# A planner that lists by latest times, and one more half-norm turned on VectorE, in a transformer layer on one core

## The chip, the cores and the metric

The kernel runs on one core of a Trainium2 chip. TensorE (PE) multiplies matrices, VectorE (DVE), ScalarE (ACT) and GpSimd (POOL) work element by element, and SyncE (SP) issues the DMAs. Each engine works through its own queue of instructions in order. The metric is the device time of one execution in microseconds (us), as a median over runs.

## The reference

A layer of 2048 rows and 640 features in fp32: a norm, attention over 8 keys at a stride of 2 (32 heads of 20), an output projection with a residual, a second norm, and a gated feed-forward network (FFN) of 1728 columns with a residual.

```python
h  = x + attention(layernorm(x), wqkv) @ wo     # keys at pos - 2*w, w = 0..7
h2 = h + (silu(n @ w_gate) * (n @ w_up)) @ w_down    # n = layernorm(h)
```

## The kernel before

The rows are worked in four blocks of 512 (`b` = 0 to 3), each in four groups of 128 rows (`j`). An fp32 product is made of three passes over splits of its operands into a high and a low part: high with high, then the two mixed ones. The high part is usually a copy on ACT, the low part a subtraction on DVE, and a transpose on PE stands ahead of both where columns are wanted.

The stages lie behind one another on PE and beside one another on the other engines: the qkv products of all blocks (L549, 480 columns wide) up to 240 us, with the projection wo(0) of block 0 (L798, 320 wide, groups of 15 matmuls) between 190 and 216 us; then the FFN of block 0 (gate and up L868, down L879, 512 wide), in which wo(1) is placed, and so on for wo(2) and wo(3). In the last part, blocks 2 and 3 share products of sums (L963, L985). The attention itself runs on DVE: products of 128x2560 (L600 and L635), sums (L607, L643), and small steps between. Its outputs are turned back to columns and split (L716, L788) ahead of each projection.

**The second norm of a block.** For every row group, `wo` adds the residual on DVE, takes the sums, forms the reciprocal deviation with short dependent steps on DVE (`rstd`, L363 to L369), and applies it on ACT. For a block in `HALF`, rows 0 and 1 are applied as a pair (`apply_pair`, L328), turned on DVE in one 128x1280 transpose (L384), stored to a scratch in DRAM with four DMAs (L388), loaded back turned (L391), and copied and split in ten pieces of 256 columns (`pair_columns`, L398 and L399); rows 2 and 3 go through ten transposes of 128x128 on PE (L407), with their copies and splits (L409, L410). For a block that isn't in `HALF`, all 20 transposes are PE's (`x_columns`, L442) with five copies (L445) and five splits (L446) of 512 columns. Before the change, `HALF` is blocks 1 and 2.

**What sets the order.** Every step is recorded in a plan with its engine, an estimated cost, what it reads and writes, and a priority number (`P.add`). `order` simulates five engines: whenever one is free, it takes the ready step with the lowest priority number. DVE's attention steps have priority 20, and wait if a step with priority 1 or less is to be ready before they would end. The start times that come out are shifted by hand for some steps (`SHIFT`, 50 entries), and the steps are emitted by these times, a step never ahead of one it depends on. What is emitted is the order of every engine's queue; no engine changes it at run time.

Of the kernel before, what the change touches and what calls it, by code (L numbers as in the profile page):

```python
# [23 lines left out]
NF = 14  # L24
# [4 lines left out]
HALF = (1, 2)  # L29
# [5 lines left out]
LAT, LAT0, RATE = 4.0, 2.0, 350e3  # L35
# [11 lines left out]
class Plan:  # L47
# [23 lines left out]
    def order(self):  # L71
        ops = self.ops
        left = [len(o[3]) for o in ops]
        succ = [[] for _ in ops]
        for n, o in enumerate(ops):
            for d in o[3]:
                succ[d].append(n)
# [7 lines left out]
        bus, loaded, start = 0.0, None, [0.0] * len(ops)  # L85
        todo = len(ops)
        while todo:
            best = None
            for e in pend:
                if ready[e]:  # L90
                    t = free[e]
                elif pend[e]:
                    t = max(free[e], pend[e][0][0])
                else:
                    continue
                if best is None or t < best[0]:
                    best = (t, e)
            t, e = best
            while pend[e] and pend[e][0][0] <= t:
                m = heapq.heappop(pend[e])[1]  # L100
                heapq.heappush(ready[e], (ops[m][4], m))
            prio, n = ready[e][0]
            if e == "PE" and prio >= 10:
                soon = min((a for a, m in pend[e] if ops[m][4] == PR["wo0"]), default=1e9)
                if soon < t + 0.3:
                    free[e] = soon
                    continue
            if prio >= 20:
                soon = min((a for a, m in pend[e] if ops[m][4] <= 1), default=1e9)
                if soon < t + ops[n][1] - 0.3:  # L110
                    free[e] = soon
                    continue
            heapq.heappop(ready[e])
            todo -= 1
            _, cost, _, _, _, table, nbytes = ops[n]
            if table is not None and table != loaded:
                cost, loaded = cost + 1.3, table
            start[n] = t
            free[e] = t + cost
            end = t + cost  # L120
            if e == "SP":
                bus = max(bus, end) + nbytes / RATE
                free[e] = max(free[e], bus - 3.0)
                end = bus + (LAT0 if ops[n][4] == 0 else LAT)
            for m in succ[n]:
                same = ops[m][0] == e and e != "SP"
                avail[m] = max(avail[m], end + (0.0 if same else 0.2))
# [3 lines left out]
        self.end = max(free.values())  # L131
        self.start = start
        left = [len(o[3]) for o in ops]
        key = [(t + SHIFT.get(n, 0.0), n) for n, t in enumerate(start)]
        heap, out = [key[n] for n in range(len(ops)) if not left[n]], []
        heapq.heapify(heap)
        while heap:
            n = heapq.heappop(heap)[1]
            out.append(n)
            for m in succ[n]:  # L140
                left[m] -= 1
                if not left[m]:
                    heapq.heappush(heap, key[m])
        return out
# [9 lines left out]
def nb(chunks, size):  # L154
    return (chunks / 16 * 0.042 + chunks * size / 435e3) * RATE


def act(n):
    return 0.155 + 0.00087 * n


def program(tc, x_in, wqkv_in, wo_in, ffn_in, ffl_in, const_in, out):
# [7 lines left out]
    with tc.tile_pool(name="sb", bufs=1) as sb, tc.tile_pool(  # L170
# [106 lines left out]
        for nm, t in (("K", ksc), ("V", vsc)):  # L277
            P.add(
                "SP", 0.07, lambda t=t: zero_halo(t), r=[rf(PROD, 1120)],
                w=[(f"{nm}{g}{a}", 0, 7) for g in range(NG) for a in range(2)], prio=6, nbytes=36e3,  # L280
            )
# [101 lines left out]
        def turn_pair(b):  # L383
            P.add("DVE", dve(1280), lambda: V.transpose(f(XN, 1280), f(XN, 1280)), r=[rf(XN, 1280)], w=[rf(XN, 1280)], prio=PR["ht"])  # L384
            for q in range(4):
                P.add("SP", 0.65, lambda q=q: Q.dma_start(
                    zsc[b, :, q, :].rearrange("(f c) t -> c f t", c=32),
                    fa[32 * q : 32 * q + 32, XN : XN + 1280].rearrange("p (f t) -> p f t", f=20)),  # L388
                    r=[rf(XN, 1280)], w=[(f"Z{b}", q, q + 1)], prio=PR["hst"], nbytes=nb(640, 256))
            P.add("SP", 0.65, lambda: Q.dma_start(f(XN, 1280).rearrange("p (k t) -> p k t", k=NC), zsc[b].rearrange("(k c) q t -> c k (q t)", c=128)),  # L390
                  r=[(f"Z{b}", 0, 4)], w=[rf(XN, 1280)], prio=PR["hld"], nbytes=nb(640, 1024))  # L391

        def pair_columns(b):
# [7 lines left out]
            for u, (n0, n) in enumerate(((10, 4), (14, 4), (18, 2))):  # L401
# [6 lines left out]
                P.add("PE", 0.115 * n, tr, r=[rf(XN + o, m), rf(IDENT, 128)], w=[pb(bk)], prio=1)  # L408
# [4 lines left out]
        def turn_rows(scratch, key, b, prio, sprio):  # L413

            P.add("DVE", dve(2560), lambda: V.transpose(f(XN, 2560), f(XN, 2560)), r=[rf(XN, 2560)], w=[rf(XN, 2560)], prio=prio)
            for q in range(4):
# [3 lines left out]
                    r=[rf(XN, 2560)], w=[(f"{key}{b}", q, q + 1)], prio=sprio, nbytes=nb(640, 512))  # L420
# [18 lines left out]
        def to_columns(u, src, srcr, dst, dstr, bk, prio):  # L439
# [3 lines left out]
            P.add("PE", 0.46, tr, r=[srcr(4 * u + q) for q in range(4)] + [rf(IDENT, 128)], w=[pb(bk)], prio=prio)  # L443
# [32 lines left out]
        def ln1(b):  # L476
# [21 lines left out]
            for j in range(NJ):  # L498
# [3 lines left out]
                for c0, n, bk, bo in ((0, 4, 7 - j % 2, 0), (4, 1, 5, j)):  # L502
# [8 lines left out]
                    P.add("PE", 0.115 * n, tr, r=[rf(XN + x0, 128 * n), rf(IDENT, 128)], w=[key], prio=1)  # L511
# [17 lines left out]
        def qkv(b, g):  # L529
# [7 lines left out]
            for j in range(NJ):  # L537
# [12 lines left out]
                for ps in [[x] for x in whole] if b == g == 0 else [whole]:  # L550
                    P.add("PE", 0.218 * len(ps), lambda ps=ps, mm=mm: mm(ps),
# [12 lines left out]
            for nmd, dst, o in (("K", ksc, so + 640), ("V", vsc, so + 1280)):  # L564
                for par in range(2):
                    P.add("SP", 0.65, lambda par=par, dst=dst, o=o: put(par, dst, o), r=[("ab", so, so + 1920)],
                          w=[(f"{nmd}{g}{par}", 1000 + 256 * b, 1256 + 256 * b)], prio=PR["kvs"], nbytes=nb(64, 2560))
                if nmd == "K":
                    P.add("SP", 0.65, lambda: Q.dma_start(qsc[b, g].rearrange("p j c -> p (j c)"), stage_t()[:, so : so + 640]),
                          r=[("ab", so, so + 1920)], w=[(f"Q{b}{g}", 0, 4)], prio=PR["kvs"], nbytes=nb(128, 2560))  # L570
# [98 lines left out]
        def turned_out(b, g, jp, src, srcr):  # L669
# [5 lines left out]
            for q in range(4):  # L675
# [4 lines left out]
                P.add("SP", 0.6, put, r=[rf(oo, 320)], w=[(f"O{b}{jp}", g + q / 4, g + q / 4 + 0.25)], prio=PR["ost"], nbytes=nb(160, 256))  # L680
# [30 lines left out]
        def last_columns(b, jp, at, sorted_, prio, rot):  # L711
# [27 lines left out]
            P.add("PE", 0.46, tr, r=[rf(last_rows(b, 2 * jp + jj), 160) for jj in range(2)] + [rf(IDENT, 128)], w=[pb(bk)], prio=prio)  # L739
# [6 lines left out]
        def wo(b, prio, bks):  # L746
# [25 lines left out]
            for j in range(NJ):  # L772
# [17 lines left out]
                for half in range(2):  # L790
# [8 lines left out]
                    P.add("PE", 2.25, mm, r=[rr(ot(5 * jp + i), 512) for i in range(5)] + [rr(WO, 6400)], w=[pb(bk)], prio=prio)  # L799
# [21 lines left out]
                if b in (0, 3) and j >= NJ - 2:  # L821
# [16 lines left out]
        def load_ffn(b, i, gu, dn):  # L838
# [17 lines left out]
            for o, at_, m in parts if b == 0 and i in KEPT else ():  # L856
                P.add("SP", 0.45, lambda o=o, at_=at_, m=m: Q.dma_start(lsc[i, :, o : o + m], r_(at_, m).bitcast(F32)), r=[rr(at_, m)], w=[(f"L{i}", o, o + m)], prio=PR["lst"], nbytes=nb(128, 4 * m))
# [7 lines left out]
        def proj(bk, gu, col, wid):  # L865
# [3 lines left out]
            for p, (w, a) in enumerate(((0, 0), (0, 1), (1, 0))):  # L869
                P.add("PE", 1.145, lambda p=p, w=w, a=a: mm(p, w, a), r=[rr(gu + 1280 * w, wid * NC), ("shb", 2560 * a, 2560 * a + 2560)], w=[pb(bk)], prio=10)  # L870
# [13 lines left out]
        def downs(batch, first, last, db=DB, cut=False, whole=False):  # L884

            for k in (4, 0, 1, 2, 3):
# [8 lines left out]
                P.add("PE", sum(3 if t[0] < NF - 1 else 2 for t in batch) * 0.229,  # L895
# [61 lines left out]
        def product(bk, terms, start, stop):  # L957

            for p, (w, a) in enumerate(((0, 0), (0, 1), (1, 0))):
# [6 lines left out]
                P.add("PE", 0.229 * n, mm, r=[z for ws, _, cs, xr in terms for z in [rr(ws[w], 256 * len(cs) - 128)] + xr(a)], w=[pb(bk)], prio=10)  # L966
# [7 lines left out]
        def plain(i, x, xr):  # L974
# [6 lines left out]
            for bk, col in ((5, 0), (6, 128))[: 2 if i < NF - 1 else 1]:  # L981
                for p, (w, a) in enumerate(((0, 0), (0, 1), (1, 0))):
# [3 lines left out]
                    P.add("PE", 1.145, mm, r=[rr(gu + 1280 * w, wid * NC)] + xr(a), w=[pb(bk)], prio=10)  # L986
# [3 lines left out]
        def early(p):  # L990
# [7 lines left out]
            for n, (bk, col) in enumerate(both):  # L998
                product(bk, [(ws(0, col), x2, (0, 1), shr)], True, False)
                P.add("ACT", act(512), lambda n=n, bk=bk: A.copy(f(EB[n], 512), banks[bk]), r=[pb(bk)], w=[rf(EB[n], 512)], prio=0)  # L1000
                P.add("SP", 0.45, lambda n=n: Q.dma_start(msc[p, n], f(EB[n], 512)), r=[rf(EB[n], 512)], w=[(f"M{p}", n, n + 1)], prio=PR["js"], nbytes=nb(128, 2048))
# [156 lines left out]
        def finish(b, db=DB, store=True, final=False):  # L1158
# [7 lines left out]
            P.add("PE", 0.46, tr, r=[rf(so, 512), rf(IDENT, 128)], w=[pb(d4)], prio=0)  # L1166
            for j in range(NJ):
                cuts = (0, 256, 512) if final and j == NJ - 1 else (0, 512)
                pieces = list(zip(cuts, cuts[1:]))[::-1]
                for o, e in pieces:  # L1170
# [9 lines left out]
                    if store:  # L1180
                        P.add("SP", 0.45, lambda row=row, o=o, e=e, j=j: Q.dma_start(out[b, :, j, o:e], row()), r=[key], prio=3, nbytes=nb(128, 4 * (e - o)))
# [152 lines left out]
```

## Time and profile before

| | |
|---|---|
| runs (us) | 845.43, 845.10, 844.89 |
| median (us) | 845.1 |
| profiled execution, its span (us) | 844.8 |
| mean granted TensorE clock | 0.999 |
| PE busy | 838.6 us, 99% |
| DVE busy | 705.3 us, 83% |
| ACT busy | 406.3 us, 48% |

The span runs from the first to the last instruction of the profiled execution, whose own time this is. A busy time counts what the profile shows as work; waits, semaphores and the issuing of DMAs are not in it. The slices of the page cut the span into 40 equal parts of 21.1 us. A chain row gives the start, the time it carried, the engine, tile and line. A timeline row gives start, length, engine, line, operation and tiles, and in brackets the idle time just before with its releaser. A row of waits gives the total, the count and the longest.

### The profile page before, as it was taken

The numbers are of one execution on the slowest core, as the hardware profiler recorded it, in microseconds if no ns is written. First come the engines' busy times: TensorE is split into PE (matmuls) and PEld (weight loads), VectorE is DVE, ScalarE is ACT, GpSimd is POOL, SyncE is SP. The second block draws the span as 40 slices with busy tenths as digits, with TensorE's granted clock in tenths as the row PEclk, the third lists the DMA queues.
The fourth block names the chain that finished last, engine by engine and source line by source line (L and its number), as shares of the span: only waits on it lengthen the run. The fifth ranks groups of instructions, "written<-read, shape, count | busy, mean of one in ns | idle before, by whom it ended". The sixth has DMA issues, their size and how long they took to land.

```text
span 844.8 us, 10863 instructions
## 1 busy us (share of the span) xinstructions
PE 838.6 (99%) x3961; PEld 712.6 (84%) x3961; DVE 705.3 (83%) x841; ACT 406.3 (48%) x674; POOL 24.5 (3%) x33
## 2 busy tenths in 40 slices
PE   9999999999999999999999999999999999999998
PEld 7888888889888888888888888888888788888886
DVE  8789999999998999999999999999434986556552
ACT  7662563244753433875434467556447543323331
POOL 0000000000000100010000010000000000000000
PEclk9999999999999999999999999999999999999999
DMA  8998598678598879577999995989933554454432
GB/s 303 272 315 250 166 243 252 185 199 239 153 282 308 269 232 333 172 218 256 305 293 302 313 277 165 254 316 309 304 111 108 185 175 157 155 170 144 153 119 84
DMA packets 91253, 191.13 MB, mean 226 GB/s; under 512 B 32560, under 2 KB 51888, under 8 KB 90560
## 3 DMA queue, kind: packets, MB, share of 16 engines
q1 hardware_dynamic: 91200, 190.44, 72.3%
q8 instruction: 31, 0.51, 0.2%
q14 instruction: 22, 0.18, 0.1%
HBM read 144.26 MB, written 46.14 MB: 225 GB/s over the span
## 4 chain that ended last, share of the span: by engine, by line
PE 92%; DVE 5%; DMA 2%; issue 1%; ACT 1%; POOL 0%; SPq 0%; DVEq 0%; POOLq 0%
PE bank L549 25%; PE bank L879 20%; PE bank L868 19%; PE bank L963 17%; PE bank L798 7%; PE bank L985 2%; DVE fa L635 1%; DMA fa<-osc 1%; PE bank L442 1%; DMA fa<-in_ffn_dram 1%; DVE fa L643 1%; PE bank L457 1%; DVE ra L788 1%; DVE fa L607 0%; DVE fa L600 0%
## 5 line engine op out<-in xcount | busy, mean ns | idle before, releaser
L868 PE MATMUL bank<-shb,ra 128*128 128x512 f32 x810 | 190.1, 390 | 0.0
L868 PEld LDWEIGHTS bank<-shb,ra 128*128 128x128 f32 x810 | 151.6, 188 | 31.0
L879 PE MATMUL bank<-ra,acts 128*128 128x512 f32 (+1 forms) x662 | 162.6, 389 | 0.0
L879 PEld LDWEIGHTS bank<-ra,acts 128*128 128x128 f32 x662 | 122.7, 188 | 24.5
L549 PE MATMUL bank<-ra,sha 128*128 128x480 f32 x480 | 106.1, 380 | 0.2 <-ACT ra L523 0.2
L549 PE MATMUL bank<-ra,shb 128*128 128x480 f32 x470 | 102.8, 379 | 0.0
L549 PEld LDWEIGHTS bank<-ra,sha 128*128 128x128 f32 x480 | 89.8, 188 | 14.2 <-ACT sha L512 0.5
L549 PEld LDWEIGHTS bank<-ra,shb 128*128 128x128 f32 x470 | 88.1, 188 | 13.1
L600 DVE TENSOR_TENSOR fa<-fa 128x2560 f32<-128x2560 f32 x32 | 90.2, 2819 | 1.8 <-DMA fa<-ksc 1.4
L635 DVE TENSOR_TENSOR fa<-fa 128x2560 f32<-128x2560 f32 x32 | 90.3, 2822 | 0.8
L607 DVE TENSOR_REDUCE fa<-fa 128x128 f32<-128x2560 f32 x32 | 90.0, 2811 | 0.5
L554 ACT ACTIVATE st<-bank,fa 128x480 f32<-128x480 f32 x64 | 42.1, 660 | 96.8 <-PE bank L549 89.3
L963 PE MATMUL bank<-shb,ra 128*128 128x512 f32 x360 | 88.1, 391 | 0.0
L963 PEld LDWEIGHTS bank<-shb,ra 128*128 128x128 f32 x360 | 67.0, 188 | 13.6 <-DVE shb L1023 0.2
L643 DVE TENSOR_TENSOR fa<-fa 128x1280 f32<-128x1280 f32 (+2 forms) x68 | 75.9, 1116 | 1.5
L1101 DVE TENSOR_TENSOR fa<-bank,fa 128x512 f32<-128x512 f32 x60 | 41.1, 690 | 43.3 <-PE bank L963 42.5
L798 PE MATMUL bank<-ra 128*128 128x320 f32 x480 | 75.0, 310 | 0.5 <-ACT fa L801 0.4
L798 PEld LDWEIGHTS bank<-ra 128*128 128x128 f32 x480 | 72.3, 188 | 3.5 <-ACT fa L801 1.3
L963 PE MATMUL bank<-ra 128*128 128x512 f32 x288 | 68.6, 390 | 0.8 <-DVE ra L1081 0.8
L963 PEld LDWEIGHTS bank<-ra 128*128 128x128 f32 x288 | 53.9, 188 | 12.5 <-DVE ra L1081 1.2
L845 ACT CAST ra<-fa 128x1280 fp32r<-128x1280 f32 (+1 forms) x38 | 45.9, 1207 | 31.4 <-PE bank L868 16.7
L913 ACT CAST acts<-fa 128x512 fp32r<-128x512 f32 x47 | 29.1, 620 | 58.9 <-DVE fa L903 33.1
(152 smaller groups left out, 845.3 us busy)
## 6 DMA issues: line engine op xcount, KB each, us to landing
fa<-in_ffn_dram SPq DMA_DIRECT2D x46, 960.0 KB, 7.7
ra<-lsc SPq DMA_DIRECT2D x45, 320.0 KB, 3.7
fa<-ksc SPq DMA_DIRECT2D x32, 440.0 KB, 7.3
fa<-vsc SPq DMA_DIRECT2D x32, 440.0 KB, 9.0
ra<-lsc SPq DMA_DIRECT2D x21, 640.0 KB, 4.9
lsc<-ra SPq DMA_DIRECT2D x13, 640.0 KB, 5.7
ksc<-st SPq DMA_DIRECT2D x32, 160.0 KB, 3.3
qsc<-st SPq DMA_DIRECT2D x16, 320.0 KB, 3.7
```

Of the source, the lines that this page charges most:

```text
L549: T.matmul(banks[bk][:, 0:480], l, r_(wq(g, w, c), 480), start=(p, c) == first_mm, stop=(p, c) == last_mm)
L554: P.add("ACT", act(480) + 0.06, lambda bk=bk, j=j: A.activation(stage_t()[:, so : so + 1920].rearrange("p (t j c) -> p t j c", t=3, j=NJ)[ ...
L600: P.add("DVE", dve(2560), lambda: V.tensor_tensor(f(PROD, 2560).rearrange("p (j w c) -> p j w c", j=2, w=W), window(ko, 2 * jp), f(qo + 32 ...
L607: P.add("DVE", dve(2560), lambda: V.tensor_reduce(f(lo + 128 * jp, 128), f(PROD, 2560).rearrange("p (n d) -> p n d", d=DH), axis=AX.X, op= ...
L635: V.tensor_tensor(f(PROD, 2560).rearrange("p (j w d) -> p j w d", j=2, d=DH), bass.AP(tensor=fa[:, vo : vo + 160].tensor, offset=fa[:, vo ...
L643: V.tensor_add(dst(v), v[:, :, 0:m, :], v[:, :, m : 2 * m, :])
L798: T.matmul(banks[bk][:, 0:320], l, r_(m, 320), start=p == 0 and c == 0, stop=p == 2 and c == NC - 1)
L845: P.add("ACT", act(n), lambda: A.copy(r_(gu, n), f(raw, n)), r=[rf(raw, n)], w=[rr(gu, n)], prio=PR["fh"])
L868: T.matmul(banks[bk], r_(gu + 1280 * w + wid * c + col, 128), x2(a, c), start=p == 0 and c == 0, stop=p == 2 and c == NC - 1)
L879: T.matmul(banks[bk][:, lo:hi], l, m, start=first and p == 0, stop=last and p == len(passes) - 1)
L963: T.matmul(banks[bk], r_(ws[w] + 256 * q, 128), x(a, c), start=start and p == n == q == 0, stop=stop and p == 2 and n == len(terms) - 1 an ...
L1101: dv(0, lambda: V.tensor_add(fb(h, dst), banks[bk], fb(h, src)), [pb(bk)] + fr(h, src), fr(h, dst))
```

## The change

It has two parts.

1. `HALF` takes in block 0. Its rows 0 and 1 then go through the pair's transpose on DVE and the scratch, with `rstd` over rows 0 and 1, and then over 2 and 3, where it was over rows 0 to 2, and then 3.
2. `order` lists three times. The first time goes by the priority numbers as before. From its order of PE's steps, `latest` computes for each step the latest time at which it may start without holding up PE, with attention steps stretched by 1.4 and DMAs by 4 us; two more listings take steps by these times. On DVE, a ready step that depends on the step taken just before it carries a penalty of 20 us, so that another one is taken where there is one. The simulated DMAs are held to eight in flight, several cost formulas have new constants, and `SHIFT` has 120 entries in place of 50.

The arithmetic of each step, the tiles and the sizes of the DMAs are as they were, beside those of block 0's second norm. In the plan there are 2811 steps after 2801. PE has 3951 instructions after 3961, DVE 845 after 841, and SP issues 593 DMAs after 588.

```diff
-HALF = (1, 2)
+HALF = (0, 1, 2)
...
-LAT, LAT0, RATE = 4.0, 2.0, 350e3
+LANES, HOP = 8, 0.035
+LAP = {"PE": 0.0, "ACT": 0.1, "DVE": 0.08, "POOL": 0.0, "SP": 0.0}
+ROUNDS = ((1.4, 20, 4.0), (1.4, 20, 4.0))
...
 SHIFT = {
-    81: -0.3, 231: -1, 232: -1, 240: 4, 308: 3, 363: 19.6, 365: 16, 375: 8, 376: -6, 387: 6.535, 389: 3.265, 541:
...
+    24: 2, 25: -16.8, 118: 1.1, 130: -1.9, 139: -20.8, 140: -29.2, 153: -102.3, 221: 8, 244: 23.7, 260: 11.8,
...
     def order(self):
+        start = self.listed()
+        for stretch, serial, dma in ROUNDS:
+            start = self.listed(self.latest(start, stretch, dma), serial)
+        self.start, self.end = start, max(t + o[1] for t, o in zip(start, self.ops))
...
+    def latest(self, start, stretch, dma):
+        ops = self.ops
+        t, due = 5.0, {}
+        for n in sorted((n for n, o in enumerate(ops) if o[0] == "PE"), key=lambda n: start[n]):
+            due[n] = t
+            t += ops[n][1]
+        last = [0.0] * len(ops)
+        for n in reversed(range(len(ops))):
+            eng, cost, _, _, prio, _, nbytes = ops[n]
+            if eng == "SP":
+                cost += nbytes + dma
+            elif eng == "DVE" and prio == 20:
+                cost *= stretch
+            last[n] = min(min((last[m] - HOP for m in self.succ[n]), default=1e9) - cost, due.get(n, 1e9))
+        return last
+
+    def listed(self, last=None, serial=0.0):
...
+            if e == "DVE" and before is not None:
+                n = min(ready[e], key=lambda x: (x[0] + serial * (before in ops[x[1]][3]), x))[1]
+                ready[e].remove((ops[n][4] if last is None else last[n], n))
+                heapq.heapify(ready[e])
+                if before in ops[n][3]:
+                    t = max(t, done[before] + HOP)
+            else:
+                n = heapq.heappop(ready[e])[1]
...
 def nb(chunks, size):
-    return (chunks / 16 * 0.042 + chunks * size / 435e3) * RATE
+    return chunks / 16 * 0.0095 + chunks * size / 323e3
+
+
+def ns(chunks, size):
+    return chunks / 16 * 0.0238 + chunks * size / 293e3
...
 def act(n):
-    return 0.155 + 0.00087 * n
+    return 0.185 + 0.00084 * n
...
-                if b in (0, 3) and j >= NJ - 2:
+                if b == 3 and j >= NJ - 2:
```

More of the change, by code (lines that the diff above doesn't have):

```diff
@@ L71, in order @@
     def order(self):
+        start = self.listed()
+        for stretch, serial, dma in ROUNDS:
+            start = self.listed(self.latest(start, stretch, dma), serial)
+        self.start, self.end = start, max(t + o[1] for t, o in zip(start, self.ops))
         ops = self.ops
         left = [len(o[3]) for o in ops]
[L74 to L77, printed above, removed]
+        key = [(t + SHIFT.get(n, 0.0), n) for n, t in enumerate(start)]
+        heap, out = [key[n] for n in range(len(ops)) if not left[n]], []
+        heapq.heapify(heap)
+        while heap:
+            n = heapq.heappop(heap)[1]
+            out.append(n)
+            for m in self.succ[n]:
+                left[m] -= 1
+                if not left[m]:
+                    heapq.heappush(heap, key[m])
+        return out
+    def latest(self, start, stretch, dma):
[14 more added lines that the diff above has]
+    def listed(self, last=None, serial=0.0):
+        ops = self.ops
+        left = [len(o[3]) for o in ops]
+        if last is None:
+            self.succ = [[] for _ in ops]
+            for n, o in enumerate(ops):
+                for d in o[3]:
+                    self.succ[d].append(n)
+        succ = self.succ
         avail = [0.0] * len(ops)
@@ L85, in order @@
         bus, loaded, start = 0.0, None, [0.0] * len(ops)
+        lanes, before, done = [0.0] * LANES, None, [0.0] * len(ops)
         todo = len(ops)
@@ L116, in order @@
             if table is not None and table != loaded:
-                cost, loaded = cost + 1.3, table
+                t, loaded = t + 1.3, table
             start[n] = t
-            free[e] = t + cost
-            end = t + cost
+            free[e] = t + cost - LAP[e]
+            end = done[n] = t + cost + (0.06 if e == "PE" else 0.0)
             if e == "SP":
-                bus = max(bus, end) + nbytes / RATE
-                free[e] = max(free[e], bus - 3.0)
-                end = bus + (LAT0 if ops[n][4] == 0 else LAT)
+                bus = max(bus, end + 1.3) + nbytes
+                end = done[n] = bus + 0.3
+                lanes.append(end)
+                free[e] = max(free[e], lanes[-LANES])
+            elif e == "DVE":
+                before = n
             for m in succ[n]:
                 same = ops[m][0] == e and e != "SP"
-                avail[m] = max(avail[m], end + (0.0 if same else 0.2))
+                avail[m] = max(avail[m], free[e] if same else end + HOP)
                 left[m] -= 1
@@ L130, in order @@
                     heapq.heappush(pend[ops[m][0]], (avail[m], m))
[L131 to L144, printed above, removed]
+        return start
 def dve(n):
@@ L279, in program @@
                 "SP", 0.07, lambda t=t: zero_halo(t), r=[rf(PROD, 1120)],
-                w=[(f"{nm}{g}{a}", 0, 7) for g in range(NG) for a in range(2)], prio=6, nbytes=36e3,
+                w=[(f"{nm}{g}{a}", 0, 7) for g in range(NG) for a in range(2)], prio=6, nbytes=0.3,
             )
@@ L894, in downs @@
                     continue
-                P.add("PE", sum(3 if t[0] < NF - 1 else 2 for t in batch) * 0.229,
+                P.add("PE", sum(3 if t[0] < NF - 1 else 2 for t in batch) * 0.227,
                       lambda k=k: [down(*t, k, first and n == 0, (last or whole and k == 3) and n == len(batch) - 1, db[k]) for n, t in enumerate(batch)],
```

62 lines of the change are left out of this document (31 added, 31 removed), and 16 rows, old and new, of the table SHIFT.

## The prediction

> **What bounds the kernel now.** I read the page first (busy shares, slices, the chain's shares), then the waits of TensorE (PE).
>
> ```profile
> span 844.8 us, 10863 instructions
> PE 838.6 (99%) x3961; PEld 712.6 (84%) x3961; DVE 705.3 (83%) x841; ACT 406.3 (48%) x674; POOL 24.5 (3%) x33
> DVE  8789999999998999999999999999434986556552
> PEclk9999999999999999999999999999999999999999
> PE 92%; DVE 5%; DMA 2%; issue 1%; ACT 1%; POOL 0%; SPq 0%; DVEq 0%; POOLq 0%
> ...
> PE bank L457 <- POOL ra L1199: 1.3, 1, 1.3
> ...
> PE bank L549 <- ACT ra L523: 0.2, 1, 0.2
> ```
>
> PE is busy 99% at a full clock and carries 92% of the chain. Its wait for the first data is 1.3 us, one for L523 just behind it 0.2, and two more stand in the timeline below. So an edit of the order can win little: the mid-run stalls, and work taken off PE. It can lose much, because VectorE (DVE) is at 90% or more from slice 4 to slice 28: if PE comes earlier to a product that DVE feeds, DVE must come earlier too.
>
> The matmul ends are modelled, so a stall is read better from start to start. The steady pace first, then the stalls, from the timeline of PE:
>
> ```profile
> 34.86 126.38 PE bank L549 x585
> 240.25 13.63 PE bank L868 x60
> 328.00 2.19 PE bank L798 x15
> 837.23 4.22 PE bank L879 x24
> ...
> 499.96 2.68 PE L798 MATMUL bank<-ra 128*128 128x320 f32 x15
> 502.48 0.86 PE L868 MATMUL bank<-shb,ra 128*128 128x512 f32 x3
> ...
> 507.68 0.84 PE L879 MATMUL bank<-ra,acts 128*128 128x512 f32 x3
> 508.93 2.47 PE L798 MATMUL bank<-ra 128*128 128x320 f32 x15 [0.42 <-ACT fa L801]
> 511.24 1.09 PE L879 MATMUL bank<-ra,acts 128*128 128x512 f32 x4
> ...
> 671.75 1.82 PE L963 MATMUL bank<-ra 128*128 128x512 f32 x7
> 674.35 3.02 PE L963 MATMUL bank<-ra 128*128 128x512 f32 x12 [0.78 <-DVE ra L1081]
> ```
>
> A 512-wide matmul costs 13.63/60 = 0.227 us, a 480-wide one 126.38/585 = 0.216, a projection group of 15 (320 wide) 2.19. So 499.96 to 502.48 is 2.52, 0.33 over 2.19; 507.68 to 508.93 is 1.25 for three matmuls (0.68), 0.57 lost; 508.93 to 511.24 is 2.31, 0.12 lost; 671.75 to 674.35 is 2.60 for seven (1.59), 1.01 lost. Together 2.0 us of mid-run stalls at three places. The run ends 844.8 - (837.23 + 4.22) = 3.4 us after PE's last matmul; in the new order PE's last two groups and the stores behind them are the same, so this tail stays.
>
> **The change part by part.** *Ten transposes.* Block 0's second norm sends rows 0 and 1 through DVE's transpose and a scratch in DRAM.
>
> ```profile
> 235.69 1.31 PE bank L442 x12
> L446 DVE TENSOR_TENSOR shb<-bank,shb 128x512 fp32r<-128x512 f32 x10 | 6.7, 682 | 3.9 <-ACT shb L445 3.9
> L384 DVE STREAM_TRANSPOSE fa<-fa 128x1280 f32<-128x1280 f32 x2 | 3.0, 1508 | 0.8 <-ACT fa L328 0.8
> L399 DVE TENSOR_TENSOR shb<-fa,shb 128x256 fp32r<-128x256 f32 x10 | 3.5, 418 | 0.0
> ```
>
> PE: twelve transposes take 1.31, so ten take **-1.1 us**, all on the path, since nothing else is PE's limit there. DVE: five subtractions of 0.682 go (3.4); one transpose of 1.508, five subtractions of 0.418, two of 512 and one of 256 columns (estimates from the rows of the same width: 0.682 and 0.418) come (5.4): +2.0 us on an engine that is full there. The four stores, the load and ScalarE's (ACT's) smaller copies lie between the projection of rows 0 and 1 and the FFN's start about 20 us later; I cost them at nothing, and at up to 1 us of PE's wait if that cover is gone.
>
> *The spacing.* In the new DVE queue 156 steps stand right behind a step that they depend on, in the old one 188.
>
> ```profile
> 226.94 0.16 DVE L365 TENSOR_TENSOR fa<-fa 128x3 f32<-128x3 f32 x1
> 227.14 0.17 DVE L366 SCALAR_TENSOR_TENSOR fa<-fa 128x3 f32<-128x3 f32 x1
> 227.54 0.16 DVE L369 TENSOR_TENSOR fa<-fa 128x3 f32<-128x3 f32 x1
> 227.64 2.30 DVE L862 TENSOR_TENSOR ra<-fa,ra 128x640 fp32r<-128x640 f32 x3
> ```
>
> L366 needs L365 and starts 0.04 after its end; L862 needs nothing of L369 and starts 0.06 before its end. Over more pairs I take 0.117 a pair (0.034 behind, 0.083 ahead): 32 fewer make 3.7 us of DVE's time, more than the +2.0. PE gains nothing by it directly; it is room. [...]
>
> *The projections come earlier.* This decides. From the order of instructions, with the paces above: PE takes the first group of wo(0) at the same place (190.7), its second half 9.7 us later (216.1), wo(1) 8.4 earlier (319.4), wo(2) 11.3 earlier (470.0), wo(3) 23.3 earlier (577.3).
>
> ```profile
> 190.38 2.82 DVE L635 TENSOR_TENSOR fa<-fa 128x2560 f32<-128x2560 f32 x1
> 193.24 2.35 DVE L643 TENSOR_TENSOR fa<-fa 128x1280 f32<-128x1280 f32 x2
> 190.85 8.79 PE bank L798 x60
> DVE shb L446 <- ACT shb L445: 3.9, 4, 2.0
> DVE fa L415 <- ACT fa L305: 2.8, 2, 2.2
> DVE fa L903 <- PE bank L868: 5.4, 10, 1.7
> 0.00:190.70 190.70, 189.15 (x881) 163.43 (x882) 176.88 (x209) 92.70 (x178) 6.33 (x13) 1.00 0.83 243
> 190.70:240.20 49.50, 49.50 (x281) 45.51 (x280) 48.06 (x54) 28.79 (x58) 3.42 (x4) 1.00 0.73 219
> 240.20:327.80 87.60, 87.60 (x388) 72.56 (x387) 82.28 (x85) 37.63 (x47) 2.26 (x3) 1.00 0.86 273
> 327.80:481.70 153.90, 153.90 (x728) 130.28 (x727) 146.02 (x147) 82.00 (x122) 6.42 (x7) 1.00 0.87 267
> ```
>
> The last four rows are stretches of the span: length, then busy time of PE, PEld, DVE, ACT. At wo(0) DVE's last split (L716) is done when L635 starts at 190.38, and PE starts at 190.85; PE needs that split only for its third pass, ten matmuls of 2.19/15 = 0.146 on, so there are 1.9 us to spare. In the new order the L635 and L643 steps that before came behind it, 2.82 + 2.35 = 5.2 us, stand ahead of it, and four dependent pairs (0.5 us) are gone: DVE must lose 5.2 - 0.5 - 1.9 = 2.8 us less than its 190.70 - 176.88 = 13.8 idle. Its waits there on ACT (L446 and L415, 6.7 us) are what can go: before, no attention step stood ahead of them. I take it that 2.5 of them go, and PE waits for the rest: **+0.3** (bounds: nothing, and 2.8 if none goes). At wo(0)'s second half 12 more steps (15.8 us) stand ahead, five pairs (0.6) fewer, and PE comes 9.7 later: with the same 1.9 to spare 3.6 of the 6.7 must go, inside the same bound. Up to wo(2) DVE is idle 481.7 - 453.2 = 28.5 us (sum of the four rows); PE comes 11.3 earlier, the queue ahead is 1.5 us shorter (15 pairs fewer), so 9.8 us of that idle time has to go. What can go is the 6.7 above and the 5.4 in which gate products (L903) wait for their matmuls, which the new order puts later in DVE's queue: 12.1, just enough. And every wait of PE before that gives DVE the same time. I put nothing here, and the bound below is a rival.
>
> *The start of the first FFN.* PE has less cover for the norm's chain: 45 matmuls of L549 (9.7 us) instead of 75 (16.2) between the last of wo(0) and the first transposes.
>
> ```profile
> 215.37 16.20 PE bank L549 x75
> 236.29 1.55 ACT L445 CAST shb<-bank 128x512 fp32r<-128x512 f32 x3
> 240.84 1.25 ACT L845 CAST ra<-fa 128x1280 fp32r<-128x1280 f32 x1
> 242.74 1.28 ACT L620 ACT_TABLE_LOAD   x1
> ```
>
> In ACT's new queue the FFN's first weight cast (L845) stands ahead of the last copy of a transposed tile. From the end of the second transpose group: two copies of 0.52, three of about 0.33 (256 wide), the cast at 1.2, the last copy 0.5, in sum 3.8 us, against 3.7 on PE (two transposes and 15 L549). A table load of 1.28 with its exponential (0.42) stands in the same stretch, if it doesn't fall before: +1.7. Bounds 0.1 to 1.8, and I take the middle: **+0.9**.
>
> *Other moves.* The stalls of the timeline above have other neighbours in the new order (the copies and splits that ended them come several steps sooner): **-2.0**, and nothing at worst. At the start the transposes of row 1 come ahead of the wait for L523: **-0.2** (the fourth wait). The moved loads keep margins near the old ones; no queue of SP (588 to 593 DMAs) holds up PE.
>
> Sum: 844.8 - 1.1 - 2.0 - 0.2 + 0.3 + 0.9 = 842.7. The median of the runs, 845.1, stands 0.3 above the profiled span: **843.0 us**.
>
> **The rivals.** *VectorE becomes the bound (slower).* PE reaches wo(2) 11.3 us earlier; if DVE regains only half of the 9.8 us it must, PE stands 4.9 us there: 843.0 + 4.9 = 847.9. At wo(3), 12 us further forward, as much again may come: 852.8. It decides from 3.8 us not regained. For: DVE at 90% or more through slices 4 to 28, its split ends 0.5 us before PE's start at wo(0). Against: 12.1 us of the waits are for ACT and PE in an order that is rewritten. Chance 0.19.
>
> *The new waits eat the gain (no change).* The ACT chain at the FFN's start takes its upper bound (+0.9 more) and wo(0) 0.7 more: 843.0 + 1.6 = 844.6. For: in a sum of 3.8 us against 3.7 a single step more is late. Chance 0.20.
>
> *The spacing is worth nothing.* If DVE's steps cost the same wherever they stand, then DVE has 21 pairs x 0.117 = 2.5 us less by wo(3), and PE stands that long: 845.5. The rows speak against it. [...] Chance 0.06.
>
> *All stalls go.* Without the 1.2 of new waits: 841.8, and some 0.8 less if half of the 1.5 us of waits at the start goes too. Chance 0.13. The forecast keeps 0.42.
>
> **How the numbers follow.** A measurement of this kernel tells 0.2% from no change, 1.7 us. Faster than 843.4: most of the forecast's case (0.36) and all of the last (0.13), with a little of the others 0.50. Within 843.4 and 846.8: 0.06 of the forecast's, 0.19, and 0.06, together 0.31. Slower: 0.19. The range leaves out the lower half of the last case and the outer half of the slower one: 841.2 to 847.9.
>
> **What would show it.** Right: PE with 3951 matmuls, L798 first starting near 190.7, 216, 319, 470 and 577 us, no wait of PE at L798 or L963 over 0.4, and DVE's waits at L446 and L903 shorter. Wrong: a wait of PE for a DVE split (L716, L788) of over 2 us at wo(1) to wo(3), or a stall of over 2 us between 230 and 242.

## The result, and the profile after

The changed kernel takes 849.4 us in the median (849.29 to 850.68), against 845.1 before: a ratio of 1.0040, with an interval from 1.0024 to 1.0057. By the medians it is 4.3 us slower (1.0051, inside that interval); the forecast was 843.0. The lines of the changed kernel are 51 higher than before's (L798 is L849, L868 is L919, L903 is L954). First lines of the page:

```profile
span 848.7 us, 10851 instructions
PE 838.7 (99%) x3951; PEld 710.2 (84%) x3951; DVE 701.8 (83%) x845; ACT 407.2 (48%) x679; POOL 25.3 (3%) x33
DVE  7999999999989999999899999996532996654552
PE 79%; DVE 14%; DMA 4%; issue 2%; ACT 1%; SPq 1%; POOL 0%; DVEq 0%; ACTq 0%; POOLq 0%
```

Then the waits of PE (total in us, count, longest):

```profile
PE bank L919 <- ACT shb L460: 1.4, 1, 1.4
PE bank L508 <- POOL ra L1250: 1.3, 1, 1.3
PE bank L849 <- DVE ra L767: 1.2, 1, 1.2
PE bank L1036 <- ACT fa L953: 0.9, 1, 0.9
PE bank L1014 <- ACT ra L1130: 0.7, 1, 0.7
PE bank L1014 <- DVE fa L1152: 0.7, 2, 0.4
```

There are ten matmuls fewer, as planned, and VectorE's busy time is 3.5 us less although the half-norm puts work on it. But beside the wait at the start (L508, 1.3 us in both kernels) there are six places at which PE now stands, for five different steps on ScalarE and VectorE. In the timeline of PE (start, length, and in brackets the idle time before):

```profile
217.26 2.02 PE L849 MATMUL bank<-ra 128*128 128x320 f32 x12 [1.21 <-DVE ra L767]
241.82 2.53 PE L919 MATMUL bank<-shb,ra 128*128 128x512 f32 x10 [1.41 <-ACT shb L460]
566.03 2.56 PE L1036 MATMUL bank<-shb,ra 128*128 128x512 f32 x10 [0.86 <-ACT fa L953]
669.60 0.97 PE L1014 MATMUL bank<-ra 128*128 128x512 f32 x3 [0.70 <-ACT ra L1130]
682.29 1.66 PE L1014 MATMUL bank<-shb,ra 128*128 128x512 f32 x6 [0.28 <-DVE fa L1152]
788.39 1.88 PE L1014 MATMUL bank<-shb,ra 128*128 128x512 f32 x7 [0.39 <-DVE fa L1152]
```

Counted from matmul end to matmul end against the steady pace, these lose 1.48, 1.65, 1.13, 0.97, 0.56 and 0.66 us. Smaller ones (192.7, 390, 395, 519, 554, 676) add 1.55. That is 8.0 us from 190 us to the end; the same count gives 2.6 before. The difference of 5.4, less 1.1 for the transposes, is 4.3, as much as between the medians. The two profiled spans differ by 3.9: the new kernel loses 0.3 less at the start, its tail is 0.3 shorter, and smaller waits make the rest.

**What sets the two stalls of block 0.** First the timeline of DVE at wo(0)'s second half, then that of ACT at the FFN's start:

```profile
213.95 0.69 DVE L767 TENSOR_TENSOR ra<-fa,ra 128x512 fp32r<-128x512 f32 x1
214.55 1.50 DVE L435 STREAM_TRANSPOSE fa<-fa 128x1280 f32<-128x1280 f32 x1
215.98 0.38 DVE L767 TENSOR_TENSOR ra<-bank,ra 128x256 fp32r<-128x256 f32 x1
216.79 0.42 DVE L767 TENSOR_TENSOR ra<-bank,ra 32x256 fp32r<-32x256 f32 x1 [0.43 <-ACT ra L766]
```

ACT in its own timeline:

```profile
236.03 0.71 ACT L449 CAST shb<-fa 128x256 fp32r<-128x256 f32 x2 [1.00 <-DMA fa<-zsc]
236.75 1.28 ACT L671 ACT_TABLE_LOAD   x1
238.37 1.05 ACT L460 CAST shb<-bank 128x512 fp32r<-128x512 f32 x2
239.32 1.03 ACT L449 CAST shb<-fa 128x256 fp32r<-128x256 f32 x3
240.24 1.26 ACT L896 CAST ra<-fa 128x1280 fp32r<-128x1280 f32 x1
241.40 0.38 ACT L460 CAST shb<-bank 128x256 fp32r<-128x256 f32 x1
```

The new turn (L435, 1.5 us) stands between the splits (L767) for which PE waits at 217.3. At 241.8 PE waits for the last copy (L460). Ahead of it in ACT's queue are the late load of the turned columns (1.0), a table load with its exponential (1.7), and the weight cast (1.2). The transposes before it ended at 237.1, so this copy is late by its place in the queue.

### The profile page after: what moved, and what is told of

It reads as the page before. It is cut to its first block, busy times and chain, and to the rows that moved or that the text cites. A ratio compares the mean times of both kernels' runs of the same rounds, so it can differ in the third digit from the quotient of the medians.

```text
span 848.7 us, 10851 instructions
## 1 busy us (share of the span) xinstructions
PE 838.7 (99%) x3951; PEld 710.2 (84%) x3951; DVE 701.8 (83%) x845; ACT 407.2 (48%) x679; POOL 25.3 (3%) x33
## 4 chain that ended last, share of the span: by engine, by line
PE 79%; DVE 14%; DMA 4%; issue 2%; ACT 1%; SPq 1%; POOL 0%; DVEq 0%; ACTq 0%; POOLq 0%
PE bank L600 21%; PE bank L930 18%; PE bank L1014 16%; PE bank L919 14%; PE bank L849 5%; DVE fa L651 3%; DVE fa L694 3%; PE bank L1036 2%; DVE fa L686 2%; DVE fa L658 2%; DMA fa<-vsc 1%; DMA fa<-in_ffn_dram 1%; DMA osc<-fa 1%; DMA fa<-qsc 1%; PE bank L508 1%
## 5 line engine op out<-in xcount | busy, mean ns | idle before, releaser
L919 PE MATMUL bank<-shb,ra 128*128 128x512 f32 x810 | 190.6, 390 | 1.4 <-ACT shb L460 1.4
L919 PEld LDWEIGHTS bank<-shb,ra 128*128 128x128 f32 x810 | 151.3, 188 | 32.5 <-ACT shb L460 1.8
L849 PE MATMUL bank<-ra 128*128 128x320 f32 x480 | 75.0, 310 | 1.2 <-DVE ra L767 1.2
L849 PEld LDWEIGHTS bank<-ra 128*128 128x128 f32 x480 | 72.1, 188 | 4.3 <-DVE ra L767 1.6
```

The source lines that it names most:

```text
L849: T.matmul(banks[bk][:, 0:320], l, r_(m, 320), start=p == 0 and c == 0, stop=p == 2 and c == NC - 1)
L919: T.matmul(banks[bk], r_(gu + 1280 * w + wid * c + col, 128), x2(a, c), start=p == 0 and c == 0, stop=p == 2 and c == NC - 1)
```

## The experiments

All ratios are against before's runs on the same chip. The line numbers shift with each kernel: the gate and up products are L919 in the changed kernel and e6, L924 in e3, L1024 in e1, e7 and e10, and L1075 in e5, e8, e9 and e11.

**e1, the half-norm alone**, in the old order, its new steps set in by hand.

```diff
-HALF = (1, 2)
+HALF = (0, 1, 2)
...
+ORDER = [ ...the old order, new steps of block 0's norm in place... ]
...
-        order = P.order()
+        P.start = order = ORDER
```

> The order of before, step for step, with only block 0's second norm changed (rows 0 and 1 turned on VectorE), its new steps set in by hand. Theory A (the loss is a sum of stalls that the new order makes, each at a place of its own; the half-norm itself is harmless): 1.1 us less for the ten transposes, at most 0.5 of new waits, so 844.0 to 844.6. Rival B (VectorE is the bound up to about 550 us, so the 2.0 us that the half-norm puts on it are paid at the next projections): 846 to 848, with waits of TensorE for L716 or L788.

0.9998 (0.9984 to 1.0011), 846.18 us against 846.19 for before on this chip: no change, so neither the gain of theory A nor the loss of rival B. PE doesn't wait for the splits that rival B named. Two of its waits:

```profile
PE bank L1024 <- DMA ra<-lsc: 1.4, 1, 1.4
PE bank L1024 <- DVE shb L566: 0.8, 1, 0.8
```

The 1.1 us of transposes are lost at the next matmul (1.04 us from end to end, at 239.8): the first FFN product writes the bank of PSUM (the memory that PE writes to) from which DVE still reads for its split (L566). And a weight load (lsc) that came in time before is late in the profiled execution.

**e2, the new order alone.**

```diff
-HALF = (0, 1, 2)
+HALF = (1, 2)
...
-                if b == 3 and j >= NJ - 2:
+                if b in (0, 3) and j >= NJ - 2:
```

> The new planner and its moves with block 0's second norm as it was (moves of steps that do not exist then are left out). Theory A: the stalls from 390 us on (together 4.8 us in the changed kernel) stay, the 1.5 us at wo(0)'s second half goes since no turn stands there, 1.1 us of transposes come back: 847.5 to 850. Rival B: VectorE has 2.0 us less to do, the later stalls shrink by as much: 845.5 to 847.

1.0349 (1.0325 to 1.0374), 30 us slower, outside both. PE stands 4.6 us at block 0's norm transposes, and the listing puts much else elsewhere. The moves are tied to the plan they were found for, so this run doesn't divide the loss into its two parts; it only shows that these moves don't carry over to a plan without the half-norm in block 0.

**e3, two places mended**: the splits ahead of the turn and of the newton steps, the exponential ahead of the copies, the weight cast behind the last copy.

```diff
+MOVES = {1031: (1019, -0.05), 1039: (1019, -0.04), 1040: (1019, -0.03), 1041: (1019, -0.02),
+         1042: (1019, -0.01), 660: (1063, -0.01), 1156: (1078, 0.01)}
...
+        for n, (m, d) in MOVES.items():
+            key[n] = (key[m][0] + d, n)
```

> The changed kernel with seven steps moved on VectorE and ScalarE alone: the last splits of wo(0)'s second half ahead of the norm's newton steps and the turn; the exponential with its table load ahead of the copies of the turned columns; the weight cast behind the last copy of a transposed tile. TensorE's order is the same. Theory A: the stalls at 217.7 (1.5 us) and 242.3 (1.65 us) go and stay gone: 846.2 to 846.8. Rival B: TensorE comes 3 us earlier to what VectorE feeds, and stands at wo(1), wo(2) or block 2's norm instead: 848.4 or more, the stalls between 330 and 570 us grown by 2 us or more.

1.0066 (1.0040 to 1.0092): no better than the changed kernel (1.0024 to 1.0057, on another chip), and by the median worse. The stall at 217 is gone, but the FFN starts at 241.56, hardly earlier than the 241.82 of the changed kernel. The timeline of PE:

```profile
241.56 6.63 PE L924 MATMUL bank<-shb,ra 128*128 128x512 f32 x21 [1.82 <-DVE shb L466]
```

Two stretches of the span (length, busy PE, PEld, DVE, ACT, POOL, and the granted clock as the third number from the end):

```profile
236.00:239.00 3.00, 3.00 (x18) 2.66 (x17) 1.47 (x4) 2.99 (x9) 0.00 (x0) 1.00 0.97 365
242.00:246.00 4.00, 4.00 (x13) 3.11 (x12) 4.00 (x6) 2.98 (x4) 0.00 (x0) 0.58 0.92 232
```

PE came earlier and waited longer, 1.1 us at the transposes and 2.1 at the FFN. Then it ran eight matmuls at half pace (granted clock 0.58 in that stretch), 1.6 us more. So the start of the FFN was not PE's to set: a chain through DVE and ACT sets it. One of the moves adds to this chain: behind the table load and the exponential, the first copy of the turned columns starts at 236.8 in place of 236.0. The time is rival B's, but not the place: between 330 and 570 us PE loses 2.1 us here and 2.3 in the changed kernel, where rival B had 2 us more.

**e4, no moves.**

```diff
-SHIFT = { ...120 entries... }
+SHIFT = {}
```

> The changed kernel with none of its 120 moves: the listing by latest times alone. If the moves heal what the listing leaves (theory A: single places), it has more and longer stalls: 853 to 870. If the listing already gives what the order can give and the moves only stir it: 848 to 851.

1.0088 (1.0060 to 1.0115), as theory A had it: the listing alone is some 4 to 5 us slower than with its moves (1.0088 against 1.0040, and medians of 854.25 against 849.41, on different chips).

**e5, the banks**: e3's order, and the FFN's first product takes over the bank of the transposes that are split first.

```diff
-                bk = (7, 6, 5)[u]
+                bk = ((5, 6, 7) if b == 0 else (7, 6, 5))[u]
```

> The kernel of e3 (seven steps moved at two places), its order kept step for step, with one thing more: in block 0 the three groups of norm transposes use PSUM banks 5, 6, 7 in place of 7, 6, 5, so that the first FFN product takes over the bank whose split is done first. In e3 that product waited for the last split but one, until 241.6 us; its last other operand was there at 239.6 and the matmul before it ended at 239.7. Theory C (the FFN's start is set by the steps on ScalarE and VectorE behind the norm, and a bank's reader is the last of them): it starts at 239.7 to 240.0, TensorE's half-speed stretch behind the stall of e3 goes, and the span is 845.5 to 847.2. Rival B (VectorE is the bound beyond): the 2 us come back as waits between 330 and 570 us, span 848 to 849.

1.0047 (1.0033 to 1.0061), span 848.7. Theory C fell: the wait at the FFN's start grew to 2.4 us. Rival B has the span, but again not the place. The timeline of PE, then those of ACT and DVE:

```profile
242.13 6.07 PE L1075 MATMUL bank<-shb,ra 128*128 128x512 f32 x19 [2.40 <-DVE shb L617]
```

```profile
235.15 1.28 ACT L827 ACT_TABLE_LOAD   x1
237.33 0.71 ACT L605 CAST shb<-fa 128x256 fp32r<-128x256 f32 x2 [0.47 <-DMA fa<-zsc]
238.07 0.43 DVE L606 TENSOR_TENSOR shb<-fa,shb 128x256 fp32r<-128x256 f32 x1 [3.27 <-ACT shb L605]
239.76 0.63 DVE L617 TENSOR_TENSOR shb<-bank,shb 128x512 fp32r<-128x512 f32 x1
241.30 1.01 DVE L617 TENSOR_TENSOR shb<-bank,shb 128x512 fp32r<-128x512 f32 x2
```

PE waits for the last but one of three splits (L617), the first of the two at 241.3. Before them, DVE stands 3.3 us for the first copy of the turned columns, which on ACT comes behind the table load, its exponential and a late load; then small attention steps stand ahead of the splits, too. So the choice of bank didn't free the first product.

**e6, the silu table early**: a one-element silu behind the exponential at 562 us.

```diff
             P.ops[n][2]()
+            if n == 959:
+                A.activation(f(LN + 119, 1), f(EPSC, 1), AF.Silu)
```

> The changed kernel, with a one-element silu on ScalarE right behind the exponential at 562 us, so that the table for silu is loaded while ScalarE is idle and not between a gate product's end (564.0) and its bank's release. Nothing else moves. Theory A (stalls are separate): the stall at 566.5 (1.1 us) goes, and stays gone: span 847.5 to 847.8. Rival B: what comes earlier waits later, at 670 or 683 us for a transfer or a combination: 848.4 to 848.8.

1.0025 (1.0016 to 1.0034). ACT in its timeline:

```profile
561.64 1.28 ACT L1340 ACT_TABLE_LOAD   x1
562.93 0.20 ACT L1340 ACTIVATE fa<-fa 128x1 f32<-128x1 f32 x1
563.44 0.60 ACT L953 ACTIVATE fa<-bank 128x512 f32<-128x512 f32 x1 [0.30 <-PE bank L1216]
```

The load falls into ACT's idle time, the wait of L1036 is gone from PE's list, and nothing grew by more than 0.25 us behind it. So this stall stood by itself. The gain fits its 1.1 us: against before's median of its own chip, this kernel loses 2.2 us, the changed one 3.4 (e12) or 4.3 (the first result).

**e7, half-norm and banks in the old order.**

```diff
-                bk = (7, 6, 5)[u]
+                bk = ((5, 6, 7) if b == 0 else (7, 6, 5))[u]
```

> The kernel of e1 (order of before, half-norm in block 0) with the banks as in e5: 5, 6, 7. In e1 the first FFN product started at 239.8 to 240.0 after 1.04 us of waiting for the split that held its bank. Theory C: that wait goes, the product starts at 239.1 or earlier, and the ten transposes are won: 0.9 to 1.2 us below before, if the load at 450 us does not come late by itself; with that wait (1.7 us in e1's profile) about as before. Rival: VectorE is full there and the next splits come late by the same amount: no change against before.

1.0002 (0.9992 to 1.0012), no change, as the rival had it. The first five matmuls of the FFN no longer wait; the sixth waits 1.0 us for another split (DVE shb L566), and loses 1.3. The wait moved on by five matmuls, and the gain with it.

**e8, e5 and e6 together.**

```diff
-        order = P.order()
+        order = ORDER      # e3's order, banks as in e5
...
+            if n == 959:
+                A.activation(f(LN + 119, 1), f(EPSC, 1), AF.Silu)
```

> e5 and e6 together. Theory A: what the two win adds up, 2.0 to 3.2 and 1.1 us below the changed kernel's span of 848.7: 844.4 to 845.6. Rival B: VectorE's queue sets the time of block 2's norm and of wo(2), and the sum is no better than the better of the two: 846.5 to 848.

1.0041 (1.0027 to 1.0055), between the two: theory A's sum isn't there. The wait at the FFN's start is 3.0 us, and 1.5 at the transposes. In its ACT timeline the copies of the turned columns begin 1.1 us after ACT is free, for their load comes late. It is issued behind a weight load that waits for DVE. That place is e3's too, but there the load was issued 0.75 us earlier and didn't hold ACT.

**e9, the norm's chain put first.** The same PE order and the same steps as e8; twelve steps are placed anew.

```diff
# n, put ahead of (b) or behind (a); several behind one step keep the order 669, 670, 671, 1158
+(1053, 1049, b), (1055, 645, b)      # row 3: copy, add
+(657, 1058, a), (658, 657, a), (659, 658, a)   # attention behind the newton steps
+(1027, 1178, b)                      # load of the turned columns
+(660, 1078, a), (1156, 660, a)       # exponential, weight cast: behind the last copy
+(669, 1068, a), (670, 669, a), (671, 670, a), (1158, 1068, a)
```

> The kernel of e8 with more steps of the chain between wo(0) and the FFN's start put first on VectorE, ScalarE and SyncE; TensorE's order is the same and no step is left out or put off by more than some 10 us: the add of row 3 and its copy come ahead of the 2.8 us attention step and of the statistics of row 2; the newton steps come ahead of the next 2.8 us step; the load of the turned columns is issued ahead of a weight load that waits for VectorE; the exponential with its table load comes behind the last copy of a transposed tile; the small attention steps behind the last splits. Theory D (the loss at the FFN's start is the place of attention steps and of one table load and one load in that chain, not VectorE's total work): the waits of e8 at 236.3 (1.7 us) and 244.0 (3.2 us) go to below 1 us together: span 842.8 to 844.5, below before. Rival B (VectorE's total work is the bound): the FFN starts earlier and TensorE waits at wo(1) or wo(2), at block 2's norm, or for gate products instead: 846 to 848.

1.0016 (1.0007 to 1.0025), span 844.6: better than the changed kernel, but 0.1 us over theory D's range, and the median (847.21) is above before's (845.76) and not below it. The timeline of PE, then that of DVE:

```profile
239.21 10.45 PE L1075 MATMUL bank<-shb,ra 128*128 128x512 f32 x45 [0.63 <-DVE shb L617]
250.53 2.79 PE L1075 MATMUL bank<-shb,ra 128*128 128x512 f32 x11 [0.87 <-DVE fa L1110]
```

```profile
247.06 2.81 DVE L814 TENSOR_REDUCE fa<-fa 128x128 f32<-128x2560 f32 x1
249.79 0.68 DVE L1110 TENSOR_TENSOR fa<-bank,fa 128x512 f32<-128x512 f32 x1
```

The FFN starts at 239.2, 2.6 us earlier than in the changed kernel (1.9 earlier than in its second profile, e12). Of that, 1.15 us comes back at 250.5: PE waits for a gate product on DVE (L1110) that stands behind a 2.8 us attention sum. Nothing came back at wo(1), wo(2) or block 2's norm, where rival B had it; it had named gate products as well, but e11 takes this wait away by moving that one product. So rival B fell as far as VectorE's total is meant; what decides is which step stands ahead of which.

**e10, the half-norm in the old order with one split ahead.**

```diff
+(1076, 1079, a)      # now ahead of two attention transposes
```

> The kernel of e7 (order of before, half-norm in block 0, banks 5, 6, 7) with one step moved on VectorE: the last but one split of the norm's columns stands ahead of two small attention transposes (0.9 us) behind which it waited. Theory D: the wait of 1.3 us at 241.4 falls to 0.3 to 0.5: 0.8 us below e7, 844.3 to 844.8 against 845.1 to 845.5 for before. Rival B: the two transposes come later, and with them the attention of block 1, whose splits end last before wo(1): no gain.

0.9996 (0.9986 to 1.0006): a tie, below e7 by less than can be told, and 845.44 us where theory D had 844.3 to 844.8. The loss behind the FFN's first five matmuls fell from 1.3 to 0.5 us, as theory D had it, but 1.1 us are lost at 447 and 458 (0.3 in e7), in part for the weight load that was late in e1 (DMA ra<-lsc 0.5).

**e11, e9 with its two largest waits mended, and a small one.**

```diff
-                bk = ((5, 6, 7) if b == 0 else (7, 6, 5))[u]
+                bk = ((6, 5, 7) if b == 0 else (7, 6, 5))[u]
+(1152, 668, b), (2170, 2249, a)
```

> The kernel of e9 with its two largest waits taken at their places: in block 0 the banks of the norm's transposes are 6, 5, 7, so that the first FFN product takes over a bank whose split is done a microsecond earlier; the first gate product stands ahead of a 2.8 us attention sum on VectorE in place of behind it; and one column sum at 679 us stands behind the gate sum for which TensorE waits. TensorE's order is that of the changed kernel. Theory D (places, not VectorE's total): the waits at 239.7 (0.9 us), 251.0 (1.15) and 679.1 (0.6) go, 2 to 2.5 us below e9: a median 1 us or more below before's of the same chip. Rival B: they turn up again at wo(1) to wo(3) or at block 2's norm: within 0.5 us of e9.

845.83 us, 1.0002 (0.9992 to 1.0013), 3.5 us below the changed kernel's 849.30 on the same chip. Theory D had it 1 us or more below before, and it ties; rival B had it within 0.5 us of e9, and by the ratios it is 1.2 us better (the intervals overlap a little). PE's waits of its profiled execution (span 842.7, the fastest of its runs):

```profile
PE bank L664 <- POOL ra L1406: 1.3, 1, 1.3
PE bank L756 <- ACT sha L719: 0.5, 1, 0.5
PE bank L1005 <- ACT fa L1008: 0.4, 1, 0.4
PE bank L1170 <- DVE fa L1308: 0.3, 1, 0.3
```

The waits at 239.7 and 251.0 are gone; 0.6 us came up at wo(1) (L1005); the one at 677 stayed (0.56, 0.59 in e9). PE starts wo(1) at 318.7, wo(2) at 470.6 and wo(3) at 579.2, which is 9.2, 11.1 and 23.6 us earlier than before, and close to the forecast's places (319.4, 470.0, 577.3). No wait for a split stands there.

**e12, the changed kernel again.** No edit.

> The changed kernel again, unaltered, for a second profiled execution and a comparison on the chip of e11. If its stalls are set by its order, the waits of TensorE at 217, 242, 566, 670, 683 and 789 us come again within 0.3 us each, and the median is 3.5 to 4.5 us over before's; if some of them are an execution's chance (a load's time), those differ by more.

849.30 us, 1.0042 (1.0026 to 1.0057), span 847.4; the median is 3.4 us over before's, just under the 3.5 to 4.5 expected. From its waits of PE:

```profile
PE bank L919 <- ACT shb L460: 1.4, 1, 1.4
PE bank L849 <- DVE ra L767: 1.1, 1, 1.1
PE bank L1036 <- ACT fa L953: 0.9, 1, 0.9
PE bank L1014 <- ACT ra L1130: 0.7, 1, 0.7
PE bank L1014 <- DVE fa L1152: 0.3, 1, 0.3
```

Five of the six stalls come again within 0.15 us: the order makes them. The sixth (788) is missing here; it comes and goes (0.97 us in e3, 0.28 in e9). With a start 0.6 us earlier it makes the 1.3 us between the two profiles.

## Why the prediction was wrong

Direction and range fail at one step: behind the FFN's start, up to the end, I took the old stalls off (-2.0) and set new waits at nothing, and there PE loses 4.7 us in place of the 0.6 that this left. New order, new stalls: at each matmul group another step can come last, and none of these was followed. The forecast's change was -2.1, the profiled spans differ by +3.9; of the 6.0 between them about 4.1 lie there, 1.3 at wo(0) and 0.75 at the FFN's start. Step by step:

- *Ten transposes, -1.1.* Right: 3951 matmuls. But they are won only if the next products can start earlier, and in the old order e1 and e7 show that they can't: a split on DVE (L566) holds them, in e1 as the reader of the first product's bank (0.8 us), in e7 ahead of the sixth matmul (1.0 us). I had written that nothing else was PE's limit there.
- *The old stalls, -2.0.* Half right. Those at 500 to 511 are gone. In place of the one at 674 there are 0.97 at 670, 0.27 at 676 and 0.56 at 683, for other steps. That a stall gets other neighbours says nothing on whether the new ones are in time. At the start (-0.2) PE does lose 0.3 less.
- *wo(0), +0.3.* Right for the first half: DVE's busy time up to 190.7 is 180.2 in place of 176.9, so it stood idle 10.5 us, where 11.0 was the most that wouldn't hold up PE, and PE lost 0.14. For the second half I counted the steps ahead of the splits as a sum, "inside the same bound"; 1.48 us were lost.
- *The FFN's start, +0.9.* The chain on ACT was the right one, with the cast and the table load in it; the price was 1.65, near the bound of 1.8 that I gave. I took the middle because the load might fall before. The load of the turned columns (1.0 us late) I had costed at nothing, and at up to 1 us "if that cover is gone". It was.
- *Everything behind, 0.* Measured 4.7 us against 2.6 before. The largest one (1.13) is a table load that falls between a gate product and its bank's release (e6 takes it away); the trace has 36 such loads in place of 34, and I didn't follow exponentials and silus in ACT's new queue past 250 us.
- *VectorE's room, the rival.* The rival's sign was right and its mechanism wrong. The spacing did more than its part: e1 and the changed kernel have the same steps on VectorE, and its busy time is 707.0 us in the old order and 701.8 in the new one, 5.2 less where I had 3.7. (That VectorE is at 90% or more "through slices 4 to 28" overlooks slice 13, at 8 tenths, and 15 pairs at 0.117 are 1.8 us, not 1.5; neither decides.) From wo(1) on PE never waited over 0.2 us for a split of a projection, though it came 5.4, 7.9 and 19.4 us earlier, and 9.2, 11.1 and 23.6 in e11. With the same PE order, and the same steps on VectorE, some twenty steps placed anew, other banks in block 0 and the early silu (e11) take the ratio from 1.0042 to 1.0002 on the same chip, 3.5 us between the medians.
- *The signs.* Neither of the two signs of being wrong came: there is no wait of over 2 us for a split at wo(1) to wo(3), and no stall of over 2 us between 230 and 242. Of the signs of being right, that of no wait over 0.4 at L798 and L963 failed, with 1.2 and 0.7. The loss is made of more and smaller waits than the forecast looked for.
- *The median, +0.3.* The runs' times are 1.7 to 2.4 us above their spans, mostly 2.1, so before's profiled execution (span 844.8) took about 846.8, which is 1.7 above the median. A run's time and a span were compared as if they were the same, and that only 0.3 lay between them is a coincidence. Before's fastest run in e11's list has a span of 842.9, 1.9 us less than the profiled one and about as much as the stalls that I took off. Whether a run at the median has these stalls, no profile shows.

What stays open: e11's profiled execution is 2.1 us shorter than before's, and the medians tie; the one is the shortest of e11's runs, the other some 1.7 us above its median. Its runs go from 844.85 to 848.11, before's from 844.86 to 848.08; what makes the longer ones was not seen in a profile. And the loss is not divided between the two parts of the change: e1 shows that the half-norm costs and wins nothing in the old order, and e2 only that these moves don't fit without it.

## What to carry to other kernels

With PE at 99%, the price of the new order was here not the sum of work ahead of each due time on the next engine (VectorE's busy time fell by 3.5 us, and the median rose by 4.3), but the place of single steps. So for each matmul group, follow who last reads its bank and who writes its operands last, and look at what stands just ahead of those steps in their queues: long steps, table loads, weight casts, a DMA issue behind a waiting one. In e3 the first of two stalls on one chain was cured (the wait of 1.2 us at wo(0)), and the second was longer (a wait of 1.8 us in place of 1.4); in e9, with the whole chain put first, it was 0.6. Cure the chain from its last link back.

## What the runs showed of the hardware

- PE ran slower behind some short stalls. After losses of 1.1 us and then 2.1 us within 7 us (e3), or 1.1 and then 2.9 (e5, 2.40 of it shown as a wait), the granted clock was 0.58 between 242 and 246 us. The next 21 matmuls took 6.63 us (e3), the next 19 took 6.07 (e5), some 1.6 us more than at 0.227 each and 0.39 for the last one: estimated from these totals, about eight of them ran at 0.427, the pace of the first matmuls of before's run (five from 3.62 to 5.75 us, where the granted clock is shown as 1.00). The changed kernel's stalls of 1.5 and 1.65 us, 24 us apart, had no such effect (the 45 matmuls from 241.82 took 10.46 us), nor had 1.7 and then 3.2 us in e8 (the seven from 243.48 took 1.85), so the length of the stalls alone doesn't tell. The slower stretch came behind gaps between matmuls of 1.8 us (e3) and 2.4 us (e5), and not in the seven matmuls behind one of 3.0 us (e8).
- In e6 a one-element activation placed a table load: it cost 0.20 us behind the 1.28 of the load, and started 0.01 behind the load's end (562.92 to 562.93).
